# A planned mLSTM and mixture-of-experts kernel: drains that wait for every GpSimd transfer in the plan, and new instruction sequences

## The chip, the cores and the metric

One Trainium2 chip, one of its cores. The metric is the device time of one execution in microseconds. Engines: PE (TensorE) multiplies, DVE (VectorE), ACT (ScalarE) and POOL (GpSimd) do elementwise work, SP (SyncE) issues most DMA transfers, and GpSimd issues indirect ones, which scatter or gather rows by a list of indices.

## What is computed

```python
for t in range(S):                      # q, k, v: (4, 8, 768, 40)
    m_new = np.maximum(f_gate[:, :, t] + m, i_gate[:, :, t])
    f_stab = np.exp(f_gate[:, :, t] + m - m_new)
    i_stab = np.exp(i_gate[:, :, t] - m_new)
    C = f_stab * C + i_stab * outer(v_t, k_t);  n = f_stab * n + i_stab * k_t
    y[:, :, t] = sigmoid(o_t) * (C @ q_t) / np.maximum(np.abs(n @ q_t), 1.0)
x = y.transpose(0, 2, 1, 3).reshape(3072, 320)
logits = x @ w_gate + modality_bias[modality_id]          # 8 experts
e_idx = argmax(logits); gate_w = softmax(logits)[e_idx]
out[mask_e] = gate_w * (np.maximum(x[mask_e] @ w1[e], 0) @ w2[e])   # w1: 320x1024, w2: 1024x320
```

## The kernel before

The recurrence is done in chunks of 128 tokens. A chunk takes the query tile qg and the states S and gives a product in Y0 or Y1 (`light`, line 1992, fp32, for the first seven pairs; later pairs in fp16 halves, where ScalarE first makes qh from qg, line 1999, and DVE the rest). `token_rows` turns a pair of chunks into normalized, gated rows, and GpSimd scatters them into a DRAM tensor x_s in the order of the experts (line 2061). Only two experts, A and B, can be chosen by nearly all tokens; a verdict word (`bword`, lines 2444 to 2451) says at the end whether that held, every engine loads it (line 2551), and a branch (line 2677) would take a general kernel if not. It isn't taken here.

The expert part runs over 14 tiles of up to 256 tokens. The tokens of the first three are picked by products with a selection matrix (lines 2188 to 2195), the others are loaded by SyncE from x_s with a transpose (line 2156). For a tile PE makes H (lines 2290, 2298), ScalarE hh (rectified, fp16, line 2278), DVE the remainder hl (line 2279), PE the output product O (line 2335; weights and activations are split into two fp16 halves, three products each), ScalarE scales O by the gate into one of three buffers ob0 to ob2 (line 2348), and GpSimd scatters ob into the output (line 2350). Up to two such stores belong to a tile.

All of this is recorded as tasks first. Each task has an engine, a duration and the names it reads and writes. A string, ORDER, holds two characters for each of the 1115 tasks and gives every engine its sequence. `Plan.run` plays these sequences through with fixed costs and gives each task a planned start. Three things hang on those starts: between which PE tasks filler products of a zz tile are put (line 2532, in planned gaps of the first 60 us), on which DVE step a GpSimd transfer has to wait (the one planned to end last before the transfer's own start; the plan keeps such transfers 2.2 us apart), and where the program is cut into two blocks. On each engine instructions then stand in the planned order and wait for what they need.

`drain()` (line 1699) is a task of GpSimd that is added after tiles 6, 9 and 11, once that tile's stores are recorded, so the plan of before starts it when these have landed. The instruction (`g_.drain()`, line 1700) names no transfer.

Of the kernel before, what the change touches and what calls it, by code (L numbers as in the profile page):

```python
# [232 lines left out]
def kernel(  # L233
# [1356 lines left out]
    "#=#>#:#X$'$&$=$<$x$y%t%u$K$M$O$a$b$d&G&H&I$S&J&K&+$g%+&*%,&P&Q%.%0&R&S&T&g&Y&Z&[%4&x&w&]&^&_'9':';'>'?'B'C'F'G'J'K'b'L'a"  # L1590
    "'M'N'O'T'U'V'W'X'Y(L%](M(N(Q(R(U(V(Y(Z(^(-(_(`(a(.%p(b(c(f(g(h(i(j(k(t(u&:)8)9):)=)>)A)B)E)F',)`)I)J)K)L)M)N)Q)R)S)T)U)V"
    ")a*#*$*%*(*K*J*)*,*-'q*0*1*4+3*5*6*7*8*9*<*=*>*?*@*A*j(=*k*l*o*p*s*t*w*x*{*|*}+8*~+#+$+'+=))+(+)+*+++,+b+c+B)p+d+g+h+k+l"
    '+o+p+s+t+u+v+w+x+{+|+}+~,#,$,8,9,:,=,>,A,B,E,F,I,J,K,L*Z,M,N,Q,R+R,S,T,U,V-A-B-C-F-G-J-K-N-O-R-S-T-U-V,)-W-Z,[-[-]-^-_-`'
    "-f-g-h-k-l-o-p-s-t-w-x-y-z-{-|.#.$.%,s.&.'.(.-.../.2.3.6.7.:.;.>.?.@.A.B.C.F.G.H.I.J.K.Q.R.S.V.W.Z.[._.`.c.d.e.f.g.h.k.l"
    ".m.n.o.p.u.v.w.z.{.~/#/&/'/*/+-8/,/-/.///2/3/4/5/6/7-=#)#,#*#?#+#/%r#U#}#2#3#4#5#<#7#I#8#J#@#A#N#B#{#K#D#L#W#C#E#M#|#F#V"
    "#G#O#Y$c#P$J$L%/$N#Q$)$-$($,$*%-$+$?$.$>$B$@$C$A$0$~$z${%#$4$1$5$F%v$G#c#f$%$|%w$}$Q%x#i%{%y$e%z$T#r&M$h&O&s&-%&$U%'#l&f"
    "&,&1&0%2#o#u&k$V&h$W$i#x$^$Y$_&.&V%5&X&}$j&~&/%6%7$`%M&4%8&5$k%~&r&z&y&{&|'='A'E%>%?'I&t$m&#%D%G'Q%@'c'h%J&j$n$Z'g'd%S(,"
    "'%%^(P%P%V'&%Y(T(](X%_%`(/'e$[$]$q%a$r(3(4&m(s'f$s%g%h%c(0%q$o%:%i%;(z&;&<$p(v(1&=&>(w(x'k'l%<)_)@%d%e({)H)<%='-,z'.)D(2"
    "&@*I(y&D&A'/&E)b'0%f&F)c)d)g'6'7)f(7&B'8(8&C'2'3*Q)e(~*P)#*'*/*L*+'r's'4*3%*'5)j(>(?*M*N*O+7)k(@(A(C(D(E't'u*n*z*v*r*T+A"
    "(G'w'x*U'{(F)*)+),'|'}'y')+H'z+D+f,|+G+C)-+j+E(H+F+n(I+r+K+L)/,<)0)q)r)s,D,@,H*[*])3)4)1)5)t)v+S)2*^)w)x+T+U+V+X)&+O*_)z"  # L1600
    "){,i*a#_(&-I-E-M-Q,*,++Y)y&u*e*f('((,](),^,,)|,-+Z,_,`*b,/,0+]-n+^+_,b-j-r,f*c,g,h,c*g,3-v,d,4,5*d,1,m,n,o,p,q,e,r,t,w,u"
    ",v,2,x(*,y.1&v,j.9.5,{+[-%-&.=-'-(-)-*-+-,--,k.^.Y,l.U.b-;-.-<-/-0-1-2.y-3-4-5-6-7/%/).}->#(###9#;#Z#y$:#z$;#[#]$/$$$v$3"
    "$E#H#b#e#h$P$R%l#q$f&L&N%%#k#n&(#t%1%3&U&W$w#w&d$X%I%L&3%}'<&`%9'@$l'D%C'H%F%R'_'P&l'$&i(K(J%m'Z%X(+($(O%O(S%U(W&)([(p(r"
    "&e'`%b)^)7)6(d'R'j*H*F);)?)[(l)C)G&?(6)O)}'1)~(}(%*&)W**(q*.)])i*2+6*:*h*i*m*B*q*u*y+`+a(B,7*S'v#^+@+%+--@-?+1+e+i,6+m+q"
    '+J+y*G,%+2,?,;).,C,G-e.+,O)u-H.,,W*`+W-D-L-d-P.P-X.s-m-i-a-q,.-u,a.O-}.).0.8.4.<.D.T.L.X.].t.a.q.i.x.|/$/(-9/0/8#1#-#.#0'
# [1075 lines left out]
```

## Time and profile before

| | us |
|---|---|
| median of three timed runs | 213.51 (212.54 to 213.6) |
| profiled execution, device time | 211.76 |
| its span, first to last instruction | 210.0 |
| PE busy | 199.4 |
| granted TensorE clock, mean | 0.989 |

The span is what the trace shows; the device time of the same execution is 1.76 us longer. A line such as L2335 is line 2335 of the kernel before. In the changed kernel the same code stands three lines lower (L2338). Names ending in q (POOLq, SPq) are an engine's queue: instructions that are not counted as busy.

### The profile page before, as it was taken

To read this page: it belongs to the slowest core of one execution; us is meant where nothing else is said; L and a number is where in the kernel's file an instruction comes from. 1 tells how busy PE (TensorE), PEld (TensorE's weight loads), DVE (VectorE), ACT (ScalarE), POOL (GpSimd) and SP (SyncE) were. 2 spreads that over 40 slices of the span, in tenths; PEclk is the share of its full clock that TensorE was granted. 3 is DMA by queue.
4 is the path that set the end of the run, shared out by engine and by line. 5 is a ranking of instruction groups with operands and counts; after the bars stand their busy time and mean duration, and the time that the engine had idled before them with its cause. 6 is when DMAs were issued, how large, how long until landed. Compare 5 with 4: busy or idle time off the path is not lost.

```text
span 210.0 us, 5305 instructions
## 1 busy us (share of the span) xinstructions
PE 199.4 (95%) x2066; PEld 156.2 (74%) x2068; DVE 130.5 (62%) x446; ACT 98.1 (47%) x202; POOL 77.6 (37%) x84
## 2 busy tenths in 40 slices
...
GB/s 194 371 378 364 385 354 274 268 332 162 124 216 83 125 34 123 129 167 238 35 65 66 148 139 155 1 5 62 34 0 38 259 301 65 0 0 65 31 54 6
DMA packets 27111, 30.72 MB, mean 146 GB/s; under 512 B 19190, under 2 KB 19480, under 8 KB 26824
## 3 DMA queue, kind: packets, MB, share of 16 engines
...
q10 hardware_dynamic: 144, 0.13, 0.2%
...
HBM read 18.57 MB, written 8.22 MB: 128 GB/s over the span
## 4 chain that ended last, share of the span: by engine, by line
PE 90%; DVE 3%; ACT 3%; issue 1%; POOLq 1%; ACTq 0%
PE O L2335 39%; PE H L2290 24%; PE H L2298 8%; PE O L2290 7%; PE Y L1992 3%; PE Y L2013 2%; PE M L2228 2%; PE O L2188 1%; PE Y L2117 1%; PE Y L2102 1%; ACT og L1972 1%; ACT junk L1973 1%; DVE sp L2479 1%; POOLq L1700 1%; PE H L1876 0%
## 5 line engine op out<-in xcount | busy, mean ns | idle before, releaser
L2350 POOL DMA_INDIRECT out<-ob,ois x25 | 25.3, 1014 | 72.7 <-ACT ob L2348 26.9
L2335 PEld LDWEIGHTS <-hh 128*128 128x128 f16 (+1 forms) x400 | 37.4, 98 | 14.7 <-issue 1.1
L2279 DVE SCALAR_TENSOR_TENSOR hl<-H,hh 128x512 f16<-128x512 f32 (+2 forms) x40 | 25.0, 645 | 36.2 <-ACT hh L2278 36.2
L2061 POOL DMA_INDIRECT x_s<-rows,pos_i x24 | 26.9, 1123 | 38.9 <-ACT hh L2278 9.7
L2278 ACT ACTIVATE hh<-H 128x512 f16<-128x512 f32 (+2 forms) x40 | 22.0, 566 | 40.6 <-PE H L2290 27.4
L2348 ACT ACTIVATE ob<-O,zs 128x320 f32<-128x320 f32 x24 | 12.4, 525 | 36.3 <-PE O L2335 21.6
L2335 PE MATMUL O<-w2hA,hh 128*128 128x320 f16 (+1 forms) x104 | 28.2, 301 | 0.0
L2335 PE MATMUL O<-w2lA,hh 128*128 128x320 f16 (+1 forms) x104 | 28.2, 300 | 0.0
L2290 PE MATMUL H<-xt,w1hA 128*128 128x256 f16 (+2 forms) x176 | 26.6, 260 | 0.0
L2335 PE MATMUL O<-w2hB,hh 128*128 128x320 f16 x96 | 26.6, 300 | 0.0
L2335 PE MATMUL O<-w2lB,hh 128*128 128x320 f16 x96 | 26.5, 299 | 0.0
L2290 PE MATMUL H<-xt,w1hB 128*128 128x256 f16 x144 | 24.4, 273 | 0.0
L2335 PEld LDWEIGHTS <-hl 128*128 128x128 f16 (+1 forms) x200 | 19.0, 98 | 7.2
L2290 PEld LDWEIGHTS <-w1hA 128*128 128x128 f16 x224 | 20.2, 98 | 3.3 <-issue 1.2
L2290 PE MATMUL H<-xt,w1lA 128*128 128x256 f16 (+2 forms) x88 | 22.2, 259 | 0.0
L2290 PEld LDWEIGHTS <-w1hB 128*128 128x128 f16 x192 | 18.0, 98 | 3.5 <-issue 1.3
L2290 PE MATMUL H<-xt,w1lB 128*128 128x256 f16 x72 | 19.6, 273 | 0.0
L2335 PE MATMUL O<-w2hA,hl 128*128 128x320 f16 (+1 forms) x104 | 15.9, 299 | 0.0
L2050 POOL TENSOR_TENSOR xr<-xr,ab 128x640 f32<-128x640 f32 x11 | 14.3, 1306 | 2.8 <-DVE ab L2033 2.6
L2335 PE MATMUL O<-w2hB,hl 128*128 128x320 f16 x96 | 15.0, 300 | 0.0
L2035 DVE SCALAR_TENSOR_TENSOR xr<-og,Y 128x320 f32<-128x320 f32 x24 | 11.2, 475 | 2.7 <-PE Y L2013 1.1
L2279 DVE SCALAR_TENSOR_TENSOR hl<-O,hh 128x512 f16<-128x512 f32 (+1 forms) x12 | 8.1, 676 | 6.5 <-ACT hh L2278 6.5
...
## 6 DMA issues: line engine op xcount, KB each, us to landing
qg<-in_ql SPq DMA_DIRECT2D x11, 384.0 KB, 5.4
...
```

The costliest lines, as they stand in the source:

```text
L1992: t_.matmul(y[p0:p1, HQ * g:HQ * g + w], lhsT=q[0:k, i, g, p0:p1], rhs=Ss[b][0:k, g, 0:w], start=(g == 0), stop=(g == 2), skip_group_check ...
L2013: t_.matmul(y[p0:p1, HQ * g:HQ * g + w], lhsT=a[0:k, i, g, p0:p1], rhs=z[0:k, g, 0:w], start=(g == 0 and t == 0), stop=(g == 2 and t == 2) ...
L2035: dve(320, lambda h=h: v.scalar_tensor_tensor(x4[:, h], og[k][:, h].rearrange("p (h d) -> p h d", h=H), 1.0, y4[h][:, :, 0:D], ALU.add, AL ...
L2050: pool(640, lambda: g_.tensor_tensor(x3, x3, ab.rearrange("p c h o -> p (c h) o").broadcast_to([P, 2 * H, D]), ALU.mult), r=abk, w=xk)
L2061: ins = g_.indirect_dma_start(out=x_s[:, :], out_offset=bass.IndirectOffsetOnAxis(ap=pos_i[:, c:c + 1].bitcast(U32), axis=0), in_=rows[:, ...
L2278: act(g * n, lambda: s_.activation(hh[:, sl, 0:n], hp3, AF.Relu), r=[nb], w=[f"hh{j}{i}" for i in fs])
L2279: dve(g * n, lambda: v.scalar_tensor_tensor(hl[:, sl, 0:n], hp3, 0.0, hh[:, sl, 0:n], ALU.max, ALU.subtract), r=[nb] + [f"hh{j}{i}" for i ...
L2290: t_.matmul(dst, lhsT=w[:, i, ws], rhs=x[:, xb], start=(first and b == 0 and q == 0), stop=(last and b == 1 and q == 2), skip_group_check= ...
L2298: t_.matmul(dst, lhsT=w[rs, place(f)[0], 2 * T:WP], rhs=x[rs, xs[r]], start=(f in fresh and q == 0), stop=(f in last and q == 2), skip_gro ...
L2335: t_.matmul(op[p0:p0 + nr, 0:DM], lhsT=t[:, at[f], o_:o_ + nr], rhs=w[:, f], start=(i < ways), stop=(i >= 24 - ways), skip_group_check=True)
L2348: act(DM + 80, lambda op=op, o=o, qc=qc, nr=nr: s_.mul(obs[o][0:nr], op[0:nr, 0:DM], facs[0:nr, qc:qc + 1]), r=[no, f"fac{m_}"], w=[f"ob{o}"])
L2350: swdma(164, lambda o=o, qc=qc, nr=nr: disjoint("outf", g_.indirect_dma_start(out=out[:, :], out_offset=bass.IndirectOffsetOnAxis(ap=ois[0 ...
```

## The change

Two things are changed. In the planner, a task may be marked `flush`. `run` keeps `land`, the latest planned landing of any GpSimd transfer issued so far, and starts a marked task no earlier. Drains are marked. And ORDER is another string, so that each engine's sequence is new. Apart from four rows of filler on PE (11,907 instructions before, 11,903 after), the instructions are the same.

```diff
-    def add(self, eng, dur, fn, r=(), w=(), kb=None, chain=None, lat=0.0, port=False):
+    def add(self, eng, dur, fn, r=(), w=(), kb=None, chain=None, lat=0.0, port=False, flush=False):
...
-        dma = port = soft_q = 0.0
+        dma = port = soft_q = land = 0.0
...
+                if t["flush"]:
+                    s = max(s, land)
...
                     f = soft_q + self.DMA_FIRST
+                    land = max(land, f)
...
-        plan.add("POOL", 0.4, lambda: g_.drain(), r, [key])
+        plan.add("POOL", 0.4, lambda: g_.drain(), r, [key], flush=True)
```

The end of GpSimd's sequence stands in this line of ORDER, of which the part up to the sign # is GpSimd's:

```diff
-    "-Y-~,}-b-c.E.*.r.j.M-:/1/9.N#$#%#'#&$9$8$t$u#~%j#`#a#d#g$#%k%o&&#p#j#m&'%n#s#v&b%A&c%H%K'~%Q%E']%B&o%W'^%Z(#%T%N&p*D%[&q"
+    "-Y-b-~,}-c.*.E.r.M.N.j-:/1/9#$#%$9#&#'$8$u$t%o%k%j#`#~#a#d&&#g$##p#m#j%n#s&'#v%A%E&c%H%B&b%K'^%W(o%T']%Q%Z'~%N&q%[&p*E*D"
```

Here the tokens .E and .M are the two stores of tile 11, .\* the second one of tile 10, .r and .j the two of tile 12 (.j the one that reads ob0), -: the store of the odd row, /1 and /9 the two of tile 13, the last tile; -c is the second drain and .N the third. Before, .N stands last, behind /9. After, it stands ahead of .j, -:, /1 and /9. The program's order as listed by the instruction rows leaves drains out, so that this line shows their place.

On PE, the place between the selections for the second and third tile (early, the trace's 16 us). Before:

```order
L2195 MATMUL O_67<-sel_166,rows 64x128
L2532 LDWEIGHTS zz
L2532 MATMUL M_68<-zz 128x512
L2532 LDWEIGHTS zz
L2532 MATMUL M_68<-zz 128x512
L2532 LDWEIGHTS zz
L2532 MATMUL M_68<-zz 128x512
L2188 LDWEIGHTS rows
L2188 MATMUL O_66<-sel_165,rows 128x64
```

And after:

```order
L2198 MATMUL O_67<-sel_166,rows 64x128
L1995 MATMUL Y_69<-S_119,qg_77 128x123 x2
L1995 MATMUL Y_69<-S_119,qg_77 128x82
L2191 LDWEIGHTS rows
L2191 MATMUL O_66<-sel_165,rows 128x64
```

Three filler products are gone, and a light chunk (three fp32 products, which the profile counts as six) that stood some 160 rows further on has their place.

On ScalarE, the first B tile and its last hh, the one out of the bank O_67. Before:

```order
L2278 ACTIVATE hh_112<-H_64 128x512
L1965 ACTIVATE w2hB<-stage 128x640
L2278 ACTIVATE hh_112<-H_65 128x512
L1973 ACTIVATE junk,zs<-og,nglo 128x640
L2278 ACTIVATE hh_112<-O_67 128x512
L1972 ACTIVATE og<-og 128x640
L1999 ACTIVATE qh_81<-qg_77 120x768
```

And after:

```order
L2281 ACTIVATE hh_112<-H_64 128x512
L2281 ACTIVATE hh_112<-H_65 128x512
L2243 ACTIVATE ex_173<-lg_171 128x16
L2002 ACTIVATE qh_81<-qg_77 120x768
L2349 ACTIVATE ob_116<-ob_116,zs 64x320
L2281 ACTIVATE hh_112<-O_67 128x512
```

The first qh, which reads a loaded qg, and one ob step now stand ahead of that hh, and qh stood two rows behind it before.

## Rows read from the trace of the kernel before

**Rows 1.** the page: busy time of each engine, share of the span, instructions.
```profile
PE 199.4 (95%) x2066; PEld 156.2 (74%) x2068; DVE 130.5 (62%) x446; ACT 98.1 (47%) x202; POOL 77.6 (37%) x84
```

**Rows 2.** the chain of waits at its end: start us, us, what.
```profile
196.44 5.54 PE O L2335 x40
...
202.25 0.51 issue
202.76 1.20 POOLq L1700
```

**Rows 3.** stretches: us, PE busy, PEld, DVE, ACT, POOL, PEclk, DMA share, GB/s.
```profile
10.00:20.00 10.00, 9.32 (x123) 7.73 (x126) 8.89 (x35) 8.02 (x18) 5.17 (x4) 1.00 1.03 372
200.00:205.00 5.00, 1.98 (x16) 1.28 (x14) 0.16 (x1) 0.53 (x1) 1.59 (x2) 1.00 0.19 57
205.00:210.00 5.00, 0.00 (x0) 0.00 (x0) 0.00 (x0) 0.00 (x0) 0.00 (x0) 0.54 0.02 6
```

**Rows 4.** the instructions of line 1700: duration min/median/max ns, first and last start.
```profile
L1700 POOLq DRAIN  x3: 3858/8229/9772, 118.4 to 202.8; - x3
```

**Rows 5.** GpSimd's timeline: start us, us, what [idle before <-releaser].
```profile
172.30 1.22 POOL L2350 DMA_INDIRECT out<-ob,ois  x1 [9.02 <-DVE sp L2400]
...
188.80 0.97 POOL L2350 DMA_INDIRECT out<-ob,ois  x1 [14.00 <-ACT ob L2348]
190.08 0.97 POOL L2350 DMA_INDIRECT out<-ob,ois  x1 [0.30 <-issue]
...
202.99 0.97 POOL L2350 DMA_INDIRECT out<-ob,ois  x1 [2.37 <-ACT ob L2348]
```

**Rows 6.** GpSimd's load of the verdict word, line 2551: ns, start us.
```profile
L2551 POOLq TENSOR_LOAD <-bword x1: 507/507/507, 206.7 to 206.7; - x1
```

**Rows 7.** the instructions of line 2677, the branch: ns, first and last start us.
```profile
L2677 SPq EVENT_SEMAPHORE  x9: 17/17/17, 206.6 to 207.2; - x9
...
L2677 POOLq INC_SWDGE_SEM  x1: 181/181/181, 208.3 to 208.3; - x1
```

**Rows 8.** SyncE's waits: us in total, times, longest.
```profile
SPq L2677 <- SPq L2677: 3.7, 1, 3.7
...
SPq L2674 <- DMA out<-ob,ois: 1.2, 1, 1.2
```

**Rows 9.** PE's timeline at the start: start us, us, what [idle before <-releaser].
```profile
13.55 1.57 PE L1992 MATMUL Y<-S,qg 120*128 120x123 f32 x12 [0.45 <-DVE ab L2028]
...
16.74 0.60 PE L2532 MATMUL M<-zz 128*128 128x512 bf16 x2 [0.16 <-issue]
```

**Rows 10.** the chain of waits, PE's light chunks and O products.
```profile
21.95 0.74 PE Y L1992 x6
...
37.21 0.83 PE Y L1992 x6
...
51.55 1.63 PE O L2335 x12
```

**Rows 11.** DMA issues: what, queue, count, KB each, median us to landing.
```profile
qg<-in_ql SPq DMA_DIRECT2D x11, 384.0 KB, 5.4
...
out<-ob,ois POOLq DMA_INDIRECT x25, 2.7
```

**Rows 12.** SyncE's DMA queue in the timeline around the last qg load.
```profile
42.41 0.64 SPq L1792 DMA_DIRECT2D qg<-in_ql  x1
```

**Rows 13.** ScalarE's timeline around the first qh: start us, us, what.
```profile
50.66 0.58 ACT L2278 ACTIVATE hh<-O 128x512 f16<-128x512 f32 x1
...
51.77 0.84 ACT L1999 ACTIVATE qh<-qg 120x768 f16<-120x768 f32 x1
...
59.55 0.55 ACT L2346 ACTIVATE ob<-ob,zs 64x320 f32<-64x320 f32 x1
```

**Rows 14.** the stretch behind the loads (columns as in rows 3).
```profile
49.00:52.00 3.00, 3.00 (x33) 2.54 (x31) 2.70 (x5) 2.91 (x7) 0.50 (x1) 1.00 0.09 36
```

**Rows 15.** the page: GB/s moved by the DMA in 40 slices of 5.25 us.
```profile
GB/s 194 371 378 364 385 354 274 268 332 162 124 216 83 125 34 123 129 167 238 35 65 66 148 139 155 1 5 62 34 0 38 259 301 65 0 0 65 31 54 6
```

More of the change, by code (lines that the diff above doesn't have):

```diff
@@ L63, in add @@
             deps[self.lead[eng]] = True
-        self.tasks.append(dict(eng=eng, dur=dur, fn=fn, deps=deps, kb=kb, lat=lat + self.LATE[eng] * (kb is None), early=self.early, port=port,
+        self.tasks.append(dict(eng=eng, dur=dur, fn=fn, deps=deps, kb=kb, lat=lat + self.LATE[eng] * (kb is None), early=self.early, port=port, flush=flush,
                                r=list(r), w=list(w)))
@@ L1589 @@
 ORDER = (
[L1590 to L1605, printed above, removed]
@@ L1606 @@
-    "#6#R#S#T$2$D$6%$$7$I%($H%|&2&7'#&6&%%)&$''&a'('i'S'n'm'[(5(e(|(9)%)h(m+4+5(:)$)P)l*R)X*;+>+?*W*C*V+&+I)m+M+N+z+.+/,&,X,P"
-    "-Y-~,}-b-c.E.*.r.j.M-:/1/9.N#$#%#'#&$9$8$t$u#~%j#`#a#d#g$#%k%o&&#p#j#m&'%n#s#v&b%A&c%H%K'~%Q%E']%B&o%W'^%Z(#%T%N&p*D%[&q"
-    ")Y(o(n&8&9'+*E)Z'*'o&n(;+<+:'p%s+9+;)')(+0(<)n*X+P,(,Z)o*Y+Q,',Y,~-#-$"
+    "#=#>#:#X$&$'$<$=$x$y%t%u$K$M$O&*$a$b$d&G&H&I&J&+&K$S%+%,%.%0&P&Q$g&R&S&T&Y&Z&g&[&]&^&_'9%4':';'>'?'B'C'F'G&x&w'J'K'L'M'N"
+    "'O'T'U'V'W'X'b'a'Y%](L(M%p(N(Q(R(U(V(Y(Z(^(_(`(a(b(c(f(g(h(i(j(-(k)8(.)9):)=)>)A)B&:)E)F(u(t)I)J)K)L)M)N)Q)R)S)T)U)V*#*$"
@@ new lines @@
+    "*%*(*)',)`*,*-*0*1)a*4*5*6*7*8*9*<'q*=*>*?*@*A*j*K*J*k*l*o+3*p(=*s*t*w*x*{*|+8*}*~+#+$+'+(+)+=+*+++,+b))+c+d+g+h+k+l)p+o"
+    '+p+s+t+B+u+v+w+x+{+|+}+~,#,$,8,9,:,=,>,A,B,E,F,I,J,K,L,M,N,Q,R,S*Z,T,U,V-A-B-C-F-G-J-K+R-N-O-R-S-T-U-V-W,)-Z-[-]-^-_-`-f'
+    "-g,[-h-k-l-o-p-s-t-w-x-y-z-{-|.#.$.%.&.'.(,s.-.../.2.3.6.7.:.;.>.?.@.A.B.C.F.G.H.I.J.K.Q.R.S.V.W.Z.[._.`.c.d.e.f.g.h.k.l"
+    ".m.n.o.p.u.v.w.z.{.~/#/&/'/*/+/,-8/-/.///2/3/4/5/6/7-=#)#2#,#{#*%r#?#+#U#/#|#3#4#5#7#<#8#V#@#I#A#N#J#K#W#D#L#B#E#Q#M#C#F"
@@ new lines @@
+    "#O#Y#G$L#P%-$N%/$($,$%$)$-$*$J$+$B$>$?$C$@$.$A$4$z$~${%#$|$}$0$5$1$F$c$G%w%v%x%z#}$Q#c#f%&%{$e%y&,%'#i&M$T#o#l#r&f&-%2&1"
+    "&0#u#x&O&V&X&.&/&h$h&k$U$V%~%G$W&#%D$^$_$`'A'E$Y%5$Z'=&y'I&~$[%6&4&z$i&{$j$k$m&}&5%M%7'Q%J%8$q%^'h%_$r%>%?%V$n$s%@%Y(P%:"
+    "%`%a%P%S(T'd&|(X'c'e(]'f$o$p$]%g%h%i'g&j(,'%'&(/(0%;(1(2&m%c(4'k%<%q(s%=(3)@'l%d%e)D&;&<&=%f)<)H(w(v&>&@&s&D&E({(x&F(z)_"
+    "(y(7(8'-'.*+'/'0*''2&r)b'3&t*/)c)d'6)g)e&A*3&B&C)f'r's'7'8(~*I)#'t'u*L*Q'{*P'|'w'})j)k+7'x'y*M*N'4*r&u*v*n*z%**O(>'5)*)+"
@@ new lines @@
+    "),+A(?(@,z+f(A(&*T*U+j+n+r+G(C+D+C'z(D)q)r)-)s)/(E(F)0)1(G(H)t(I+E+F+H+K+L)z,<,D)3)4,@,|)5,H'))2*[*])&*^*_*a*b-E)v+S+T+U"
+    ")w-I*e*f+V){)|*g)x-M-Q,*,++O,i,,+X+Y,j,-,/(',3+Z-j-r+]+[,]-n+^+_-v,^,_,`*c)y,0,4,1,b,5,c,f,g,d,m*d,n,o,h,p,q,r,t,w.5,e,u"
+    ",v((().1.=.9.U.Y-%-&-'.^.b-(-),2-*-+-,--#_-.-/,y,x-0(*,k-1-2-3-4-5.y-6-7.}&v/),l-;-<,{/%->#(###9$$#;$:#y#Z#[#]#z$v#H$3$;"
+    "%l$/$E#b#e$P$R%%#h#q#n$f&L#k#t%1&(&N#w%F&W&U%3&d%C$w%}%L&l'@$X'D%I'<&`'H&3%m%R'_%X'P$l&)(p(J(K%9(+%U%O(O&i*F'Z(S(W%b(r'R"
```

4 lines of the change are left out of this document (added).

## Prediction

> **What bounds the kernel now.** I read the page's shares first, then the chain that ended last, then the stretches, and then the places that the change touches. PE is busy for 95% of the span [rows 1]. A high share alone would not prove that it is the bound, but the chain shows it: from the start of its third group of light products at 13.55 us [rows 9] on, PE runs without a break worth naming to 196.44 + 5.54 = 201.98 us, and only then come the verdict word, 0.51 us in which the engines load it, and GpSimd's drain of L1700 [rows 2]. The stretches say the same: PE fills all of 10 to 20 us, 1.98 us of 200 to 205, and nothing after [rows 3]. So there are two places in which time can be had: in PE's stream (its work, its fillers and its waits, nearly all before 60 us), and in the 8 us behind its last matmul. An engine that is reordered elsewhere costs or gives something only if PE comes to wait for it.
>
> **The tail, term by term.** The three drains last 3.86, 8.23 and 9.77 us, and the last one begins at 202.8 [rows 4]: the moment at which GpSimd has the last store in hand, which it issues at 202.99 for 0.97 us [rows 5]. The drain ends 202.76 + 3.86 = 206.62. Only then does GpSimd load the verdict word (0.51 us, from 206.7) [rows 6] and leave by the branch, and its last step there, at 208.3 + 0.18, is 1.86 us behind the drain's end [rows 7]. The other engines did the same at 202.25 to 202.76 [rows 2]. SyncE resets its semaphores from 206.6 to 207.2 [rows 7] and then waits 1.2 us [rows 8]. That wait is put down to the store, but the store has landed by then (it was issued at 202.99 and stores land in 2.7 us [rows 11]; the drain, which waits for it, ends at 206.62): it ends at 208.4 with GpSimd's last step.
>
> After the change the last drain stands in front of the last four stores and none follows the last store. GpSimd then takes the word at 202.99 + 0.97 = 203.96 and is through with its 1.86 us at 205.8, while the store is still landing. SyncE's start at 206.6 I leave where it is, since the store has to land all the same. What goes is the wait of 1.2 us: **-1.2**. The bounds: 0, if what SyncE waits for at 207.2 is something else than GpSimd's step; and, if its 3.7 us of standing still before 206.6 [rows 8] also end with the drain and not with the store, it could begin when the store lands, 202.99 + 2.7 = 205.7, another 0.9 earlier: -2.1. I take -1.2 because it has a row of its own. The Trainium skill (DMA: Bandwidth & Descriptors, "Anatomy of one DMA — SWDGE (gpsimd) path") gives a GpSimd transfer 2.0 us fixed plus its bytes over 436 GB/s, most of the fixed part being the write's receipt, which no order of instructions takes away; for this store of 164 KB that makes an estimate of 2.4 us, and the lower bound would be -2.4 by it instead of -2.1. The trace's 2.7 us is the same kind of cost, somewhat larger.
>
> **The drains in the middle.** In the trace a drain lasts as long as the transfers under way, 3.9 to 9.8 us, where the plan of before let it start when its own tile's two stores had landed. The new plan knows the rest too, but the instruction is the same. What is queued behind a drain is GpSimd's next store, and behind that an ob buffer. The last drain now stands between the stores of tiles 11 and 12: where before stores went at 188.80 and 190.08 [rows 5], now two go at 188.8 and about 191 (the plan keeps 2.2 us between them), the drain waits until the second has landed, 1 + 2.7 us [rows 11], and the store of ob0 that left at 190.08 leaves at about 195. ScalarE writes ob0 again when PE's last product is there, at 202. 195 + 1 + 2.7 = 198.7 is early enough, with a cover of 3.3 us: 0.
>
> **PE's start.** In the trace PE stands between its first select products and those of the second tile from 16.58 to 17.34, 0.16 us idle and 0.60 us of zz filler [rows 9]; the plan of before has three filler products there, that of after has one light chunk (three fp32 products of line 1992) in their place. That chunk ran at 21.95 for 0.74 us [rows 10]; next to other shapes such a chunk takes up to 0.83. So 0.74 goes later and 0.83 - 0.76 = 0.07 comes in: -0.67, if the wait for the selection is not longer than before. Other fillers of the first 16 us shrink or grow too, but a filler fills a wait that the plan expects, so its going is worth nothing by itself: 0.
>
> Against it: DVE, ScalarE and SyncE have new orders in the first 16 us. The row of zeros on DVE goes ahead of the scans, token rows and selections change places, one gate load goes ahead of another. No trace shows these orders. The nearest row is the one real wait of PE in that stretch, 0.45 us for DVE's ab at 13.55 [rows 9]. None of these adds work, so one such wait about covers it: between 0 and three of them, 1.35; I take 0.3.
>
> Between 36 and 39 us two light chunks stand singly between the half-array products of line 2335, each 0.83 us [rows 10]. They now stand together, behind the half-array run. A lone chunk costs 0.09 more than 0.74 (0.83 against 0.74), and each return to the half array delays the next product about as much: -0.2 for both, between 0 and -0.4.
>
> PE together: -0.67 + 0.3 - 0.2 = -0.57; I take **-0.5**, between -1.1 and +1.3. The clock is 1.00 up to 205 us [rows 3] and there is no idle stretch to lose it in.
>
> **The sum.** -1.2 - 0.5 = -1.7 us, against the profiled execution's own 211.76 us, that is 210.1. The three timed runs have a median of 213.51, 1.75 us more than the profiled one; the same difference goes off it: 213.51 - 1.7 = 211.8, said as **211.9**, since the uncertain terms of PE's start lean to the dear side.
>
> **The rivals.**
> Tail alone. PE's new waits eat what the chunk gives (three waits of 0.45 instead of 0.3 us), so PE ends where it did or 0.5 later: 213.51 - 1.2 + 0 to 0.5 = 212.3 to 212.8, or 213.0 if the tail gives nothing and PE alone the 0.5 (the change then does not do what it says: the end hangs on the store, not on the drain). For it: every engine's order in the first 16 us is new and untested by this trace.
>
> ScalarE's line, slower. ScalarE takes instructions in order. In the middle of the first B tile it now makes qh from qg (line 1999 of before, 0.83 us) and one ob ahead of the last hh of that tile; before, that hh was done first, at 50.66, and qh followed at 51.77 [rows 13]. PE's O products wait for this hh. qg's load is one of the last of the stream: the last one of it went out at 42.41 [rows 12] and lands 5.4 us later [rows 11], at 47.8; by 49 the DMA has nothing left (share 0.09 from there) [rows 14]. If it lands at 49, then 49 + 0.83 + 0.55 (an ob of that form) + 0.58 (hh) = 51.0 [rows 13], against 50.66 + 0.58 = 51.2 before: no loss, with 0.2 us to spare and what PE can do without that hh, some 1.6 us (12 products [rows 10]). It decides from a landing at about 51 on; each us after that is a us of the end. The loads run at 268 to 385 GB/s, changing by slice [rows 15]. Were they 10% slower over 49 us, the last would land near 54 and cost some 3 us: 213.51 - 1.7 + 3 = 214.8. Against it: the bytes are the same, and the DMA share is about 1 up to there in any order. The Trainium skill (the same page, "Queues, rings and completion order") says that each DMA engine serves its queue rows in turn, packet by packet, so a GpSimd store of 168 KB beside qg's load would push it back by its own bytes: at 373 GB/s an estimate of 0.45 us a store, one or two of which still fit before 51.
>
> The last drain holds the stores. If it lasts as long as the longest, 9.8 us [rows 4] instead of 3.7, ob0's store slips by 6.1 us, 2.8 more than its cover: 213.51 - 1.7 + 2.8 = 214.6. The longest stands in the gap of 9.02 us ahead of the store at 172.30 [rows 5], where the DMA moved 259 and 301 GB/s (163 to 173 us); from 189 to 194 it moved 65 [rows 15]. Small.
>
> The whole tail hangs on the drain: -2.1 - 0.5 = -2.6, 210.9.
>
> **How the numbers follow.** Forecast 0.50 (211.2 to 212.4); whole tail 0.08; tail alone or PE alone 0.26; ScalarE's line 0.13; the last drain 0.03. No change is what lies within 0.5% of 213.51, 1.07 us: from 212.44 to 214.58, about what a measurement can tell. Faster 0.50 + 0.08 = 0.58, same 0.26, slower 0.16. The range takes in the whole tail with PE's better bound on the low side (213.51 - 2.1 - 1.0 = 210.4) and, on the high side, a ScalarE stall of half the price on top of PE's three waits (213.51 - 1.2 + 0.5 + 1.5 = 214.3).
>
> **What would show it.** Right: no drain behind the last store; GpSimd's load of the word near 204 instead of 206.7 and no SyncE wait of 1.2 us; the end 1.2 us nearer to PE's last matmul; a light chunk of line 1995 instead of filler near 16.7, and every later PE step about 0.5 us earlier. Wrong: SyncE's wait still there, with another releaser; PE waits over 0.5 us between 8 and 25 us, or at the O products near 51 us for hh, with qh before it on ScalarE; the last ob waiting for a store.

## The result, and the profile of the kernel after

The change makes the kernel slower by about 1.5 us: 214.62 us in the median (213.97 to 215.37) against 213.26 us, a ratio of 1.0072 with an interval of 1.005 to 1.0095. The forecast was 211.9 us, faster. The sign was wrong, and the time lies above the range. Ratios here leave disturbed executions out, the medians given with them do not.

Built with the old ORDER, the planner's new rule gives the instruction stream of the kernel before, row for row. All that follows comes from the new sequences. Line numbers of the new kernel are 3 higher than before (2335 is now 2338).

The profiled execution took 214.62 us, with a span of 212.5. First the tail. The groups of the drain, the load of the verdict word and the branch (duration min/median/max in ns, first and last start in us), then SyncE's wait:

```profile
L1703 POOLq DRAIN  x3: 4806/5116/5332, 135.7 to 193.8; - x3
...
L2554 POOLq TENSOR_LOAD <-bword x1: 505/505/505, 206.5 to 206.5; - x1
...
L2680 SPq EVENT_SEMAPHORE  x9: 17/17/17, 210.2 to 210.8; - x9
...
L2680 POOLq INC_SWDGE_SEM  x1: 272/272/272, 210.4 to 210.4; - x1
...
SPq L2680 <- SPq L2680: 3.9, 1, 3.9
```

The three drains lie between 135.7 and 199, none behind the last store [rows 4]. GpSimd loads the word at 206.5, 1.1 us behind PE's end of 205.40; before, it was 4.7 us behind (206.7 against 201.99) [rows 6]. SyncE still stands 3.9 us before its resets, which begin 3.5 us behind the last store's issue at 206.75 (3.6 before, 206.6 against 202.99 [rows 5]), but its wait of 1.2 us behind them [rows 8] is gone: GpSimd's last step (210.4) now comes before SyncE's last reset (210.8), where it came 1.1 us after it [rows 7]. From PE's end to the span's end it is 212.5 - 205.40 = 7.1 us; before it was 210.0 - 201.99 = 8.0, and in four more executions of the kernel before 8.2 to 8.4. The tail did what was forecast.

PE did not. Its waits in the new kernel, by line and releaser (us in total, times, longest):

```profile
PE O L2338 <- ACT ob L2351: 1.2, 1, 1.2
...
PE O L2191 <- DVE rows L2049: 0.9, 1, 0.9
PE O L2338 <- ACT hh L2281: 0.4, 1, 0.4
...
PE M L2231 <- DVE lg L2236: 0.2, 1, 0.2
...
PE Y L1995 <- DVE xr L2038: 0.2, 1, 0.2
```

Behind the first light product these are some 3 us; before there were 0.45 + 0.16 = 0.6 [rows 9]. The longest lies where the prediction didn't look at all. The stretch around it (us, PE busy, then PEld, DVE, ACT, POOL, clock, DMA share, GB/s):

```profile
70.00:100.00 30.00, 28.79 (x312) 23.00 (x311) 20.13 (x59) 11.53 (x24) 15.62 (x15) 1.00 0.51 120
```

PE is full in every stretch from 100 to 205 us (105.00 of 105.00), but here it misses 1.21 us.

### The profile page after: what moved, and what is told of

It is laid out like the page before. It is cut to its first block, busy times and chain, and to the rows that moved or that the text cites. A ratio compares the mean times of both kernels' runs of the same rounds, so it can differ in the third digit from the quotient of the medians.

```text
span 212.5 us, 5286 instructions
## 1 busy us (share of the span) xinstructions
PE 200.7 (94%) x2065; PEld 157.3 (74%) x2066; DVE 133.8 (63%) x446; ACT 98.9 (47%) x202; POOL 74.9 (35%) x84
## 5 line engine op out<-in xcount | busy, mean ns | idle before, releaser
L2353 POOL DMA_INDIRECT out<-ob,ois x25 | 24.7, 988 | 68.9 <-ACT ob L2351 20.4
L2064 POOL DMA_INDIRECT x_s<-rows,pos_i x24 | 25.4, 1059 | 43.7 <-ACT hh L2281 7.5
L2057 DVE TENSOR_TENSOR rows<-xr,rows 128x128 f16<-128x128 f32 (+1 forms) x22 | 10.5, 494 | 7.0 <-ACT rows L2055 7.0
L2236 DVE TENSOR_REDUCE lg<-M 128x16 f32<-128x32 f32 (+2 forms) x14 | 2.5, 178 | 15.8 <-PE M L2231 15.8
```

What stands on the lines that cost most here:

```text
L2057: two(2 * (z - a0), lambda a0=a0, z=z, o=o: v.tensor_tensor(rows[:, cs, o:o + z - a0], xr[:, :, a0:z], rows[:, cs, a0:z], ALU.subtract), r ...
L2064: ins = g_.indirect_dma_start(out=x_s[:, :], out_offset=bass.IndirectOffsetOnAxis(ap=pos_i[:, c:c + 1].bitcast(U32), axis=0), in_=rows[:, ...
L2236: dve(16 * nh, lambda: v.tensor_reduce(lg, M0[0:n, 0:16 * nh].rearrange("p (h a e) -> p h e a", h=nh, a=2), axis=AX.X, op=ALU.add), r=["M0 ...
L2353: swdma(164, lambda o=o, qc=qc, nr=nr: disjoint("outf", g_.indirect_dma_start(out=out[:, :], out_offset=bass.IndirectOffsetOnAxis(ap=ois[0 ...
```

## The wait at 84 us: a DVE step of 0.17 us that lasts 2.78

The timelines of four engines around 84 us in the new kernel (start us, us, what, idle before and its releaser). PE, then ScalarE, DVE and GpSimd:

```profile
84.11 0.30 PE L2338 MATMUL O<-w2hA,hh 128*128 128x320 f16 x1 [1.21 <-ACT ob L2351]
...
83.43 0.21 ACT L2243 ACTIVATE ex<-lg 128x16 f32<-128x16 f32 x1 [1.65 <-DVE lg L2242]
83.55 0.51 ACT L2351 ACTIVATE ob<-O,zs 128x320 f32<-128x320 f32 x1
...
80.62 2.78 DVE L2242 TENSOR_TENSOR lg<-lg,mxx 128x16 f32<-128x16 f32 x1
...
80.10 0.97 POOL L2353 DMA_INDIRECT out<-ob,ois  x1 [1.21 <-DVE lg L2239]
81.09 1.06 POOL L2111 TENSOR_TENSOR aw<-aw,bT 128x512 f32<-128x512 f32 x1
82.09 1.27 POOL L2053 TENSOR_TENSOR xr<-xr,ab 128x640 f32<-128x640 f32 x1
```

Read from below. GpSimd does two elementwise products back to back, 81.09 to 83.36. The DVE step of line 2242, 16 numbers a partition, starts at 80.62 and ends at 83.40, with the second of them. ScalarE takes its instructions in order: ex waits for that step, ob stands behind ex, and PE's next O product waits for ob to leave its bank. The same step in the group of its line in the new kernel (min/median/max ns), then the same line before (there 2239):

```profile
L2242 DVE TENSOR_TENSOR lg<-lg,mxx x14: 150/168/2782, 34.0 to 160.3; 128x16 f32<-128x16 f32 x11, 128x8 f32<-128x8 f32 x2, 64x8 f32<-64x8 f32 x1
```

```profile
L2239 DVE TENSOR_TENSOR lg<-lg,mxx x14: 145/166/177, 27.6 to 147.4; 128x16 f32<-128x16 f32 x11, 128x8 f32<-128x8 f32 x2, 64x8 f32<-64x8 f32 x1
```

Thirteen of fourteen are as short as before; one is held. Theory: GpSimd's elementwise steps hold the DVE step, and PE pays. Rival: PE's start and ScalarE's order at 54 us make the loss, and this hold is a bystander. The first experiment makes GpSimd's aw (line 2111, task 746) wait for the DVE step (task 377), so that they change places; it stands where the tasks are emitted:

```diff
+    kept = {}
...
         made = t["fn"]()
...
+        kept[i] = made
+        for late, soon in [(746, 377)]:
+            if i == late:
+                tc.add_manual_dep(made.ins, kept[soon].ins.name, mybir.DependencyInfo(mybir.DependencyClass.Sync, mybir.DependencyReason.DATA),
+                                  reason="the port")
```

> The changed kernel, with one more wait: GpSimd's second addition to aw (line 2111) waits until DVE has subtracted the row maximum from the logits of the same moment (line 2242). In the trace of the changed kernel that DVE step starts at 80.62 and lasts 2.78 us instead of 0.17, until GpSimd's two elementwise steps behind it are done, and PE then waits 1.21 us at 84.11 for a bank that ScalarE frees behind that step. Theory (GpSimd's two-input step keeps DVE out): the DVE step is over before 81.2, PE's wait of 1.21 us falls to under 0.3, and the end comes 0.9 to 1.2 us earlier than the changed kernel's 214.6. Rival (what PE waits for there is late for another reason, or another wait takes its place at once): the DVE step or the PE wait stays above 0.8 us, the time within 0.3 us of 214.6.

Measured: 213.0 us, ratio to the kernel before 0.9997 (0.997 to 1.0023). One wait, added on GpSimd, takes back 0.0075, 1.6 us; that this is more than the wait of 1.21 us is within the two intervals. DVE in that kernel, then GpSimd (its profiled execution, 214.33 us, is the longest of the ten):

```profile
81.51 0.18 DVE L2242 TENSOR_TENSOR lg<-lg,mxx 128x16 f32<-128x16 f32 x1
...
82.20 2.09 DVE L2244 SCALAR_TENSOR_TENSOR ky<-lg,cst 128x16 f32<-128x16 f32 x1
...
80.99 0.97 POOL L2353 DMA_INDIRECT out<-ob,ois  x1 [1.21 <-DVE lg L2239]
81.98 1.06 POOL L2111 TENSOR_TENSOR aw<-aw,bT 128x512 f32<-128x512 f32 x1
82.98 1.27 POOL L2053 TENSOR_TENSOR xr<-xr,ab 128x640 f32<-128x640 f32 x1
```

The step runs in 0.18 us, and the hold has moved to the next DVE step with two operands, ky, which again ends with xr (84.29 against 84.25). Nothing on PE's path waits for ky: the O product follows at 83.63 with no idle time. So the hold belongs to GpSimd's two products, not to line 2242, and what it costs depends on which DVE step it meets. The store's own step (0.97 us) holds nothing: line 2242 ran inside it.

The Trainium skill (SBUF — State Buffer, "Who interferes with whom") says that DVE and GpSimd share a pair of SBUF ports, that a DVE instruction with two SBUF inputs contends with a GpSimd instruction that reads SBUF, and that the pair is an exclusive lock: of DVE's two-port modes it says that whoever issues first gets the pair for the whole instruction and the other fully blocks. The rows agree: lg and mxx are two such inputs, and 2.78 us is the wait for aw and xr.

The planner knows this pair. It marks line 2242, the rows and the selections (`two` in the kernel), like all of GpSimd's steps but the drains, as users of one port, and never plans two of them at once. Played through, the plan starts aw just when line 2242 ends. But a planned start isn't a wait: in the program nothing keeps GpSimd back when DVE comes later than planned, until the experiment adds it.

The second experiment leaves the hold and takes PE's bank out of it: ScalarE does ob ahead of ex.

```diff
-    "(['$($)[)6)7(d'j)?)C(l);)^)G&e*H&?)~)O)}(6***&*.'1)W*2*h(}+1*:*i'v*B*m+6)i*q*u*y+%+@'`+a(%+`*S+e+i,6(B+-+m-@,7+q+y+J,%,;"
+    "(['$($)[)6)7(d'j)?)C(l);)^)G&e*H&?)~)O)}(6***&*.)W'1*2*h(}+1*:*i'v*B*m+6)i*q*u*y+%+@'`+a(%+`*S+e+i,6(B+-+m-@,7+q+y+J,%,;"
```

> The changed kernel with one pair swapped on ScalarE: the ob step (line 2351) ahead of the exponential (line 2243) that waits for DVE's L2242. GpSimd and DVE are left as they are. Theory (the 2.78 us in which DVE is kept out reach PE only through ScalarE's line, where ob stands behind ex): L2242 still lasts over 2 us, PE's wait of 1.21 us at 84 falls under 0.3, and the time falls by 0.9 to 1.5 us, as with the wait for L2242 (213.0). Rival (DVE's later hl steps are what PE needs next): a wait of PE for hl takes its place, time 214.2 or more.

Measured: 214.17 us, ratio 1.0052 (1.0024 to 1.008). DVE, ScalarE and PE there:

```profile
80.10 2.78 DVE L2242 TENSOR_TENSOR lg<-lg,mxx 128x16 f32<-128x16 f32 x1
...
81.17 0.52 ACT L2351 ACTIVATE ob<-O,zs 128x320 f32<-128x320 f32 x1
...
86.09 0.45 PE L2338 MATMUL O<-w2hA,hl 128*128 128x320 f16 x2 [0.72 <-DVE hl L2282]
```

ob is early, its wait is gone, and 3.9 us behind the first of these O products (82.22) PE waits 0.72 us for hl: DVE itself is late by the hold. Freeing one consumer of a held engine returns only the difference to the next; the interval doesn't tell this kernel from the change.

## The selected rows at 17 us

PE waits 0.9 us there for DVE's rows (line 2049). DVE, GpSimd and PE in the new kernel:

```profile
15.14 1.89 DVE L2049 TENSOR_TENSOR rows<-xr,rows 128x64 f16<-128x64 f32 x3
...
15.30 1.45 POOL L2053 TENSOR_TENSOR xr<-xr,ab 128x640 f32<-128x640 f32 x1 [0.48 <-DVE rows L2049]
...
17.09 0.28 PE L2191 MATMUL O<-sel,rows 128*128 128x128 f16 x2 [0.91 <-DVE rows L2049]
```

Of line 2049's four steps the longest takes 1481 ns; before, the longest took 418. GpSimd's xr runs beside it. Making xr wait for line 2049 should have freed it (the same edit as at 84 us, with xr's task 183 and the rows' task 105):

```diff
+        for late, soon in [(183, 105)]:
```

> The changed kernel, with one more wait: GpSimd's third product xr (line 2053, 15.30 us) waits until DVE has written the low parts of the first chunk's rows (line 2049). One of these lasts 1.48 us in the changed kernel and at most 0.42 before, and PE waits 0.91 us at 17.09 for it. Theory (the same hold): line 2049 lasts at most 0.45 us everywhere, PE's wait of 0.91 falls below 0.2, later PE steps come 0.7 to 0.9 us earlier, the time about 213.8. Rival (DVE's new order of the token rows is itself what comes late): the wait stays above 0.6, time within 0.3 us of 214.6.

Measured: 214.99 us, ratio 1.0057 (1.0023 to 1.0092), no gain that can be told (the clock, told with the three edits below, has a part in that). DVE, GpSimd and PE:

```profile
16.55 1.29 DVE L2171 TENSOR_SCALAR sel<-iota_f,posf 128x192 f16<-128x192 f16 x1
...
16.51 1.26 POOL L2053 TENSOR_TENSOR xr<-xr,ab 128x640 f32<-128x640 f32 x1 [1.23 <-DVE rows L2049]
...
18.50 0.28 PE L2191 MATMUL O<-sel,rows 128*128 128x128 f16 x2 [1.09 <-DVE rows L2057]
```

xr went 1.2 us later and met the selection of line 2171 instead, on the same path: the wait grew from 0.91 to 1.09. So xr was put behind the rows of line 2057 as well (task 127), where the plan has it too:

```diff
+        for late, soon in [(183, 127)]:
```

> The changed kernel with GpSimd's third product xr (line 2053) held until DVE has written all low parts of the first two chunk pairs' rows (both L2049 and L2057), since with a wait for L2049 alone the hold moved to L2057 (1.09 us of PE's time instead of 0.91). Theory (the product of GpSimd in that place, not DVE's order, costs PE the 0.9 us): no row step on DVE is stretched, PE's wait ahead of the second tile's selections is under 0.2 us, the time 213.7 against the changed kernel's 214.6, if the rows of the next pair, which now come some 1.5 us later, are not missed. Rival (they are missed): a new wait of PE of 0.5 us or more between 18 and 35 us, time 214.3 or more.

Measured: 214.14 us, ratio 1.0035 (1.0004 to 1.0065), against 1.0072 for the change: a gain at the edge of what the intervals tell. Where this hold goes is seen in the kernel of three edits, below.

## ScalarE's line at 54 us: the rival that came true in part

ScalarE in the new kernel:

```profile
52.58 0.84 ACT L2002 ACTIVATE qh<-qg 120x768 f16<-120x768 f32 x1 [0.78 <-DMA qg<-in_ql]
...
53.78 0.57 ACT L2281 ACTIVATE hh<-O 128x512 f16<-128x512 f32 x1
...
54.41 0.31 PE L2338 MATMUL O<-w2hB,hh 128*128 128x320 f16 x1 [0.41 <-ACT hh L2281]
```

qh waits for its load, an ob step and hh stand behind it, PE waits 0.41 us. With qh and ob behind that hh, as before:

```diff
-    "%l$/$E#b#e$P$R%%#h#q#n$f&L#k#t%1&(&N#w%F&W&U%3&d%C$w%}%L&l'@$X'D%I'<&`'H&3%m%R'_%X'P$l&)(p(J(K%9(+%U%O(O&i*F'Z(S(W%b(r'R"
-    "(['$($)[)6)7(d'j)?)C(l);)^)G&e*H&?)~)O)}(6***&*.'1)W*2*h(}+1*:*i'v*B*m+6)i*q*u*y+%+@'`+a(%+`*S+e+i,6(B+-+m-@,7+q+y+J,%,;"
+    "%l$/$E#b#e$P$R%%#h#q#n$f&L#k#t%1&(&N#w%F&W&U%3&d%C$w%}%L&l'@$X'D%I'<&`'H&3%m%R'_%X'P$l&)(p(J(K%9(+%U%O(O&i*F'Z(S(W%b([(r"
+    "'R'$($)[)6)7(d'j)?)C(l);)^)G&e*H&?)~)O)}(6***&*.'1)W*2*h(}+1*:*i'v*B*m+6)i*q*u*y+%+@'`+a(%+`*S+e+i,6(B+-+m-@,7+q+y+J,%,;"
```

> The changed kernel with ScalarE's first qh and the ob step behind it put back behind the last hh of the first B tile, as they stood before. The changed kernel's PE waits 0.41 us there, at 54.41, for that hh. Theory (ScalarE's order, the prediction's slower rival): that wait goes, and the time falls by 0.4 us if nothing fills it. Rival (hh is late for its own reasons, or a later wait absorbs the 0.4): the wait stays, or it goes and the end moves by less than 0.2 us.

Measured: 214.28 us, ratio 1.0046 (1.0018 to 1.0074). ScalarE there:

```profile
52.76 0.60 ACT L2281 ACTIVATE hh<-O 128x512 f16<-128x512 f32 x1 [0.61 <-PE O L2293]
53.25 0.83 ACT L2002 ACTIVATE qh<-qg 120x768 f16<-120x768 f32 x1
```

PE's wait at this place is gone. In the traces of the variants that keep the new order it is 0.28 to 0.75 us in four and absent in two; a second trace of the change itself (below), in which it was expected again, doesn't have it either. That qh ahead of hh delays hh is the rival's mechanism. That the load's landing sets the size isn't shown: in the trace of the first experiment qh has no wait of its own and PE waits 0.73 us, in the second trace of the change qh waits 0.51 and PE not at all. The price was some 0.5 us, not 3.

## Three and four edits together

The wait on lg, the wait on both rows and the old place of hh in one kernel:

```diff
+        for late, soon in [(183, 127), (746, 377)]:
```

> The changed kernel with three small edits together: the wait for L2242 (which alone gave 213.0), the first qh back behind the last hh of the first B tile (214.3 alone), and GpSimd's third xr behind both row steps. Theory (the three waits of PE add up, and the tail's gain stays): 211.8, between 211.3 and 212.3, faster than the kernel before by 0.4 to 0.8%. Rival (the waits replace one another): 212.6 to 213.2.

Measured: 212.2 us, ratio 1.0004 (0.9966 to 1.0043). PE's waits in its trace from 7.5 us on, then the place of the largest on DVE, GpSimd and PE:

```profile
PE Y L1995 <- DVE xr L2038: 1.4, 2, 1.2
PE M L2231 <- DVE lg L2236: 0.6, 1, 0.6
```

```profile
16.19 1.19 DVE L2035 TENSOR_SCALAR ab<-ab 128x16 f32<-128x16 f32 x1
...
16.09 1.26 POOL L2053 TENSOR_TENSOR xr<-xr,ab 128x640 f32<-128x640 f32 x1 [2.22 <-DVE rows L2057]
...
17.82 0.90 PE L1995 MATMUL Y<-S,qg 120*128 120x123 f32 x6 [1.18 <-DVE xr L2038]
```

The waits at 84, at 54 and for the selected rows are gone, and xr, later again, holds a step of 0.17 us for 1.19, in front of the very light chunk that was to fill PE's gap. The waits sum to 2.0 us, against 3.06 in the change and 0.6 before. Seven of its ten executions lie from 211.85 to 212.47, one at 213.01 and two at 214.8. Their clock may part them: the two have a mean granted clock of 0.982, the seven 0.989 to 0.992. No trace caught one of the two, but the kernel with xr behind line 2049 has a wait of PE at the same place (1.09 us, up to 18.50), and in its trace the granted clock fell behind it; from 20 to 24 us it was 0.57 (third column from the end), most of that time at the 1.2 GHz level, where the change has 1.00:

```profile
20.00:24.00 4.00, 4.00 (x51) 3.68 (x48) 3.17 (x9) 2.68 (x5) 1.77 (x2) 0.57 1.03 358
```

From the light chunk at 19.24 to the M product at 34.28 PE took 15.0 us there, in the change 13.6 (18.82 to 32.44): 1.4 us more for the same work and waits. The trace with both rows (1.18 us of wait, an execution of 216.25 us) shows the same fall. The four kernels whose traces have such a wait (1.09 or 1.18 us: both edits of the rows, the three and the four edits) are the ones of which two to five executions lie 1.4 us or more above all others of the same kernel, so a wait of PE there can cost more than its length. It doesn't do so each time: the traces of the three and the four edits have the wait and no fall.

A fourth edit adds modb's old place on DVE (its reason is told in the section on PE's start):

> The three small edits that gave 212.2 together (GpSimd's second addition to aw behind L2242, the first qh behind the last hh of the first B tile, GpSimd's third xr behind both row steps) and modb ahead of G. Theory (all four losses of the changed kernel are found, its gains remain): the runs near 214.8 that the three showed (2 of 10) go, median 211.6 to 212.1, faster than the kernel before by 0.4 to 0.7%. Rival (the clock's rise is chance): median 212.2 to 212.6 with such runs still there.

Measured: 212.38 us, ratio 0.9982 (0.9937 to 1.0028): equal to the kernel before within the interval. Three of its ten executions lie at 214.3 to 214.5, with a mean granted clock of 0.981 to 0.982, so modb's place doesn't take such executions away. By the traces the new sequences, mended at their three losses, have the tail's gain and still lose most of it on PE.

## The tail alone

Undoing only the drain's move in the new kernel (.N back behind /9):

```diff
-    "-Y-b-~,}-c.*.E.r.M.N.j-:/1/9#$#%$9#&#'$8$u$t%o%k%j#`#~#a#d&&#g$##p#m#j%n#s&'#v%A%E&c%H%B&b%K'^%W(o%T']%Q%Z'~%N&q%[&p*E*D"
+    "-Y-b-~,}-c.*.E.r.M.j-:/1/9.N#$#%$9#&#'$8$u$t%o%k%j#`#~#a#d&&#g$##p#m#j%n#s&'#v%A%E&c%H%B&b%K'^%W(o%T']%Q%Z'~%N&q%[&p*E*D"
```

> The changed kernel with the third drain put back to the end of GpSimd's sequence, behind the last store. Theory (the tail term of the prediction is right and hidden under losses elsewhere): the word is loaded by GpSimd only after a drain of about 3.9 us, SyncE's wait of 1.2 us is back, and the time rises by 0.9 to 1.2 us over the changed kernel's 214.6. Rival (the drain behind the last store costs nothing, the end hangs on the store's landing): within 0.3 us. Second rival (the drain ahead of the last four stores is what made the change slower): 0.5 us or more faster.

Measured: 216.29 us over four executions, ratio 1.017 (1.0134 to 1.0206), 2.1 us slower than the change. Its drains and GpSimd's steps at the end:

```profile
L1703 POOLq DRAIN  x3: 3816/5377/5410, 134.5 to 204.6; - x3
...
L2554 POOLq TENSOR_LOAD <-bword x1: 506/506/506, 208.7 to 208.7; - x1
...
L2680 POOLq EVENT_SEMAPHORE  x6: 17/30/43, 211.1 to 211.5; - x6
...
L2680 POOLq COMPARE_BRANCH  x1: 64/64/64, 209.3 to 209.3; - x1
```

The drain is back at the end, the word is loaded at 208.7, and here the step from the branch to GpSimd's first event takes 1.8 us (before it took 0.5, 207.2 to 207.8), which goes with a price larger than in the kernel before. The change's own two traces have 1.3 and 1.8 us at this step, but there it lies beside the store's landing and SyncE's start doesn't wait for it. Why it is longer in the new kernel is open.

The reverse, and the version to keep: the kernel before, with nothing but the last drain moved ahead of the last stores.

```diff
-    "-Y-~,}-b-c.E.*.r.j.M-:/1/9.N#$#%#'#&$9$8$t$u#~%j#`#a#d#g$#%k%o&&#p#j#m&'%n#s#v&b%A&c%H%K'~%Q%E']%B&o%W'^%Z(#%T%N&p*D%[&q"
+    "-Y-~,}-b-c.E.*.r.j.M.N-:/1/9#$#%#'#&$9$8$t$u#~%j#`#a#d#g$#%k%o&&#p#j#m&'%n#s#v&b%A&c%H%K'~%Q%E']%B&o%W'^%Z(#%T%N&p*D%[&q"
```

> The kernel before, with one token moved: the third drain goes from the end of GpSimd's sequence to behind the second store of tile 11, ahead of the odd row's store and the last tile's two. Nothing else is reordered. Theory (the tail term is right by itself): GpSimd loads the word before the last store's landing, SyncE's wait of 1.2 us is gone or under 0.3, and the time is 1.0 to 1.7 us under the kernel before (213.0). Rival (the drain was free there, and the 1.7 us that the changed kernel lost with its drain put back came from something else): within 0.4 us of 213.0.

Measured: 211.36 us (210.88 to 212.46), ratio 0.9942 (0.9917 to 0.9967): faster than both kernels, by 1.2 us than the one before. The groups:

```profile
L1700 POOLq DRAIN  x3: 3139/7848/9908, 119.1 to 192.5; - x3
...
L2551 POOLq TENSOR_LOAD <-bword x1: 513/513/513, 202.8 to 202.8; - x1
...
SPq L2677 <- SPq L2677: 3.3, 1, 3.3
```

PE ends at 201.99 as before [rows 2], the word is loaded 3.9 us earlier [rows 6], and the span ends 7.2 us behind PE. The tail's term is measured here with nothing else changed.

## PE's start, and why one trace is not enough

The two traces compared first differ in one more thing. The first row below is the change's profiled execution, the second another execution of the same kernel, the third another one of the kernel before:

```profile
6.48 1.59 PE L1879 MATMUL H<-kvs,kws 64*120 64x123 f32 x12
```

```profile
6.36 0.90 PE L1879 MATMUL H<-kvs,kws 64*120 64x123 f32 x12 [0.30 <-DVE kws L1868]
```

```profile
6.19 0.90 PE L1876 MATMUL H<-kvs,kws 64*120 64x123 f32 x12 [0.34 <-DVE s L1913]
```

The same twelve products take 0.90 or 1.59 us. The filler products around them differ in the same way: of 512 columns, two take 0.56 us and three 0.78 in the fast traces, 0.94 and 1.37 in the slow one, so that one more adds 0.22 or 0.43. That is half the speed, as 1.2 GHz is half of 2.4; no row names the level, since the stretch from 0 to 8 us has a granted clock of 1.00 in the change's first trace (the column behind POOL's) as in the others:

```profile
0.00:8.00 8.00, 6.45 (x30) 3.06 (x30) 5.74 (x34) 2.65 (x5) 3.44 (x17) 1.00 0.73 231
```

PE had products and fillers ahead of them in either case. The light products then start at 7.7 to 7.9 or at 8.9 to 9.2. I first took this for an effect of the change: on DVE modb had moved behind another early step, and PE's first products wait for it. Put back in the new kernel, and put in place in the old one:

```diff
-    ".m.n.o.p.u.v.w.z.{.~/#/&/'/*/+/,-8/-/.///2/3/4/5/6/7-=#)#2#,#{#*%r#?#+#U#/#|#3#4#5#7#<#8#V#@#I#A#N#J#K#W#D#L#B#E#Q#M#C#F"
+    ".m.n.o.p.u.v.w.z.{.~/#/&/'/*/+/,-8/-/.///2/3/4/5/6/7-=#)#2#,#{#*%r#?#+#U#/#|#3#4#5#<#7#8#V#@#I#A#N#J#K#W#D#L#B#E#Q#M#C#F"
```

> The changed kernel with one DVE step moved: the cast modb stands ahead of the scan G, as in the kernel before, instead of behind it (the fillers of the first 5 us follow the plan: 437 and 291 columns instead of 512, 217 and 182). In five of seven traces with the changed start, 512-column fillers still take 0.44 us each at 8 us and the first products H take 1.59 us for twelve; in all three traces with the old start they take 0.90 us. In the changed start PE waits 0.29 us at 4.71 for modb; in the old one it has no break before 4.52. Theory (that break at 4.4 to 4.7 us costs the early rise of TensorE's clock in most executions, and some 1.3 us with it): PE has no wait at 4.7, H takes 0.90 us, the time falls by 0.6 to 1.3 us to 213.3 to 214.0. Rival (when the clock rises is chance and doesn't hang on that break): time within 0.4 us of 214.6, H at 1.59 us in most traces.

> The reverse on the kernel before: modb behind G, nothing else (fillers 512, 217 and 265 columns instead of 437 and 475). Theory (the break ahead of 4.7 us delays the clock's rise): PE waits some 0.3 us at 4.7 for modb, the twelve products H take 1.59 us in the trace, and the time rises by 0.6 to 1.3 us over 213.0, with a wider spread of the runs. Rival (chance): H takes 0.90 us, the time within 0.4 us of 213.0.

Measured: 214.33 us, ratio 1.0057 (1.0026 to 1.0087), and 212.65 us, ratio 0.9979 (0.9951 to 1.0007). Neither edit moves its kernel beyond the interval; the late modb doesn't slow the old one. That theory fell. More executions of both kernels, unedited, show it:

> The kernel before once more, unchanged, for its trace. In the profiled execution of before, the twelve first products H took 0.90 us and the light products began at 7.72; in the changed kernel's 1.59 us and 9.17, with the same shapes, and in the changed kernel with the drain put back 0.90 us and 7.89, though its first 60 us are the same as the changed kernel's. Theory (when TensorE's clock rises in the start differs from one execution to the next, whatever the order): this trace may show either; if it shows 1.59 us, its span is 1.2 to 1.5 us over the 210.0 of the first, near 211.4. Rival (the old order always has the early rise): 0.90 us and about 210.0 again.

> The kernel before, unchanged, for its first 10 us. Up to now the old start shows an early rise of TensorE's clock (0.90 us for the twelve products H) in three of three traces, and a fourth with modb late; the changed kernel's start shows it in three of eight, not counting those with modb early. Theory (the new start misses the early rise more often than the old): 0.90 us again. Rival (the two starts don't differ, and the old one was lucky): 1.59 us in at least one of three looks.

> As before_look2, a second look: 0.90 us if the old start has the early rise always, 1.59 us in some if it is chance.

> As before_look2, a third look: 0.90 us if the old start has the early rise always, 1.59 us in some if it is chance.

> The changed kernel, unchanged, a second look at its trace. Its waits of PE at 17, 54 and 84 us (0.91, 0.41, 1.21) belong to the order and come again within 0.3 us each whatever the clock does in the start; the twelve products H may take 0.90 or 1.59 us, and the span follows with some 1.3 us.

Measured: 212.51, 213.17, 212.07, 214.0 and 214.04 us. The products took 0.90, 1.59, 0.90 and 1.59 us in the four of the kernel before, 0.90 in that of the change. It differs by execution with both sequences; what decides it stays open. It moves the start of the light products by 1.2 us, and in the execution of 214.0 us the first 24 of them were slow too, 3.71 us instead of 3.02. That is most of what the executions of the kernel before spread (211.82 to 214.31), and the two traces compared first had it on opposite sides.

Like with like, from the timelines of PE (us; waits are those behind the first light product; "rest" is PE's end less its waits less the light products' start):

| trace | first light product | waits | PE's end | rest | to the span's end |
|---|---|---|---|---|---|
| before, 212.07 us | 7.72 | 0.62 | 202.01 | 193.67 | 8.3 |
| before, drain early | 7.72 | 0.46 | 201.99 | 193.81 | 7.2 |
| after, 214.04 us | 7.89 | 3.29 | 204.84 | 193.66 | 7.1 |
| after, ob first | 7.89 | 3.27 | 204.40 | 193.24 | 7.1 |
| after, three edits | 7.89 | 2.01 | 203.28 | 193.38 | 6.9 |
| after, four edits | 7.89 | 1.81 | 202.66 | 192.96 | 7.1 |
| before, first trace | 7.72 | 0.61 | 201.99 | 193.66 | 8.0 |
| after, first trace | 9.17 | 3.06 | 205.40 | 193.17 | 7.1 |

Between the first and the third row PE ends 2.83 us later: 0.17 by its start, 3.29 - 0.62 = 2.67 by its waits, the rest nothing. The tail gives 1.2 back, and the span grows by 1.6 us. That is the result. Of the 3.29 us of waits in the third row, 0.92 are for the rows at 16 us and 1.22 for the bank at 83; 0.57 are for line 2236's lg at 32 us, where DVE is late behind another held step. In the change's first trace, with 0.20 us of that wait, it is this one:

```profile
30.37 1.26 DVE L2035 TENSOR_SCALAR ab<-ab 128x16 f32<-128x16 f32 x1
...
30.31 1.28 POOL L2053 TENSOR_TENSOR xr<-xr,ab 128x640 f32<-128x640 f32 x1
```

The three make 2.71 us, and what is left, 0.58, is no more than before. No experiment freed the step at 30 us, so its part is argued.

## Why the prediction was wrong, point by point

**The tail: right.** SyncE's wait of 1.2 us is gone, and SyncE's start, with no drain behind the store, still came 3.5 us after the store's issue in the change and 206.2 - 203.00 = 3.2 in the old kernel with the early drain (3.6 before): it hung on the store's landing for the most part. The old kernel with the drain alone gains 1.2 us by its ratio; the whole-tail rival (-2.1) is out.

**The drains in the middle: right.** They last 4.8 to 5.3 us, and the store behind the last one leaves at 199.50, not 195 (of the 4.5 us between, 3.4 are those by which PE is late altogether). Its buffer is free again, by the 1 + 2.7 us of [rows 5, 11], at 203.2, and ScalarE's last ob begins at 205.44, when PE is done. The rival of the held stores didn't come true, although the cover was thinner than worked out.

**The chunk in the gap: half.** The chunk stands there, but waits for DVE itself: 0.17 us in the two traces of the change, 1.18 in the kernel of three edits. The rest of PE's stream is shorter by 0 to 0.7 us (193.66 to 193.81 in the traces of the old sequences above, 192.96 to 193.66 in those of the new), where chunk and half-array switches were to give 0.87. No experiment moved the chunk alone, so how this divides is open.

**PE's new waits: the step that failed.** The term was +0.3, at most 1.35; it measured +2.7. It was sized by the one wait that the old trace showed, on the ground that "None of these adds work, so one such wait about covers it" (the 0.45 us of [rows 9]). Moving work changes what runs beside what, and two engines that hold each other make a DVE step longer without adding any: 0.17 to 2.78 us at 80 us, 0.42 to 1.48 at 15 us. The first experiment shows it: one wait on GpSimd, and 1.6 us come back. At 15 us the edits moved the hold and PE's wait with it, but didn't end the loss. And it was sized for the first 16 us and the half-array run alone, while the dearest wait lay at 84 us, where GpSimd's sequence had moved, and where I had asked only which queue its drains hold. The old trace had the warning, a held DVE step off PE's path:

```profile
30.82 1.84 DVE L2236 SCALAR_TENSOR_TENSOR lg<-lg,bias 128x8 f32<-128x8 f32 x1
...
30.13 2.49 POOL L2050 TENSOR_TENSOR xr<-xr,ab 128x640 f32<-128x640 f32 x2
```

Its line has a median of 174 ns.

**ScalarE's line: a rival that came true in part.** In the change's first trace hh stood behind a qh that waited 0.78 us for its load. It cost 0.28 to 0.75 us where it cost at all, and undoing it gave 0.55 us by the ratios, less than their intervals.

**The reference.** The execution that the sum was made against was one with the early start of the light products, and 211.76 us is less than any timed execution of that kernel in the later comparisons (the lowest took 211.82). Taking the difference to the median off again was right, but a comparison of two single traces, which the prediction offered as its test ("every later PE step about 0.5 us earlier"), carries 1.2 us of chance.
